# Block-sparse attention with channel mix on one core: another fixed order of the same 2139 operations

## The chip, the cores and the metric

One core of a Trainium2 chip runs the kernel in one launch. The metric is the device time of one execution in microseconds (us), the median over runs. Engines are called as the profile calls them: PE (TensorE), DVE (VectorE), ACT (ScalarE), POOL (GpSimd) and SP (SyncE, which here only issues transfers).

## The reference

What is computed, cut to its core:

```python
scores = scale * q @ k.T            # batch 4, heads 8, sequence 768, head size 64
mask = window(+-1 block of 32) | first/last block row | first/last block column | 3 drawn blocks per row
attn = exp(where(mask, scores, -1e9) - max); attn = attn / (sum(attn) + 1e-9)
x = (attn @ v) as [4, 768, 512]
x_prev = x shifted by one token
xk = mu_k * x + (1 - mu_k) * x_prev;  xr = mu_r * x + (1 - mu_r) * x_prev
k = maximum(xk @ w_k, 0);  v = (k * k) @ w_v      # w_k 512x1024, w_v 1024x512, w_r 512x512
out = sigmoid(xr @ w_r) * v
```

## The kernel before

The sequence has 24 blocks of 32 tokens. The attention is cut into 26 units. Units 0 to 21 ("near") are block rows 1 to 22, each for all four batches: eight blocks of keys (window, first and last block, three drawn ones). Units 22 to 25 ("wide") are the first and last block row of one batch each, against the whole sequence.

A near unit goes through these steps, each one an entry of the plan: its query tile (L305), one new window block of keys (L284) and three drawn blocks (L332) are loaded by SP into slots of a resident tile `KA`, the values in the same way into `VA` (L297, drawn ones L349). PE computes scores in two halves (L402), DVE the row maxima (L412, `nm`), ACT the exponentials (L452, `p`), DVE transposes blocks of 32 (L455, `r`), SP moves the result between partitions by four DMAs (L463, "move", `pt<-r`), PE multiplies with the values (L475). Units 0 to 3 transpose on PE instead (L371, values at L436). Wide units do the same at L496 (scores), L526 (move) and L538 (values), with their own keys (L310) and values (L314). Then the division (L557, L567), a transpose (L576), another move (L581, `xm<-rx`) and a copy into the token tile `xt` (L586, L587, "put x").

The channel mix runs over twelve tiles of 256 tokens, in the order 1 to 10, 0, 11. For each: the two token-shift mixes (L666 on ACT, then L673 on DVE or L669 and L670 on POOL), split into a high and a low part so that three matmul passes give the product (L685, L688, L689); the gate r (L716, in halves `r<t>_0` and `r<t>_1`), the hidden layer h (L737, four pieces `h<t>_0` to `h<t>_3`, ReLU at L752, square and split at L753 to L760), the sigmoid (L805), the values v (L772, eight matmul groups a piece), the product (L778) and the store (L781). The weights come as 64-bit numbers, 0.52 MB a tile (L187, `raw<-w_k` and the like), and are split on chip (around L246).

Nothing is scheduled by a tool. The program builds a list `plan.ops` of 2139 operations, and `Plan.order` hands them out in the sequence of the table `ORDER`; each engine executes its own operations in just that sequence, and waits at an operation until its inputs and its buffers are ready. SP's list is such a sequence too: a move that waits for a transpose holds back all loads behind it. The table `CHOICE` says, by the name of an operation, which engine does it, where several can (`choose`):

```python
def order(self):
    assert sorted(ORDER) == list(range(len(self.ops)))
    return [self.ops[i] for i in ORDER]
...
engine, ns, port, fn = ways[CHOICE.get(name, 0)]
```

`KA` and `VA` are used as rings: a load into a slot has to wait until the unit that read the slot has done so. `r` and `pt` have few buffers, so a unit's transposes follow the move of the one before.

Of the kernel before, what the change touches and what calls it, by code (L numbers as in the profile page):

```python
# [95 lines left out]
def block_sparse_attention_channel_mix(  # L96
# [770 lines left out]
}  # L867
ORDER = [
# [130 lines left out]
```

## Time and profile before

| | us |
|---|---|
| median of 3 runs | 519.79 |
| lowest and highest | 517.22, 520.74 |
| profiled execution | 523.44 |
| its span | 521.7 |
| PE busy in the span | 481.9 (92%) |
| DVE, ACT, POOL busy | 314.0, 306.2, 229.9 |
| mean granted clock of PE | 0.98 |

The span is what the hardware profiler saw of one execution, from the first to the last instruction; the execution's own time is 1.74 us more. The profiled execution lies 3.65 us above the median. A row of a timeline has the start, the length, the engine with the line of the kernel, the output and the input, and in brackets how long the engine stood idle before it and what ended that. A row of a table of waits has the waiting engine and line, what released it, the sum, the count and the longest.

### The profile page before, as it was taken

How to read it: one execution, taken by the hardware profiler on the slowest of the kernel's cores; microseconds unless marked ns; L12 is line 12 of the kernel's file. 1: busy time of each engine (PE TensorE's matmuls, PEld its weight loads, DVE VectorE, ACT ScalarE, POOL GpSimd, SP SyncE). 2: the span in 40 equal slices, each digit the busy share in tenths (PEclk: the TensorE clock that was granted, in tenths of full speed). 3: DMA queues.
4: the chain of work that ended last, by engine and by line, in shares of the span. 5: the costliest groups of instructions: out<-in, count | busy, mean ns of one | idle time of the engine just before them, and what ended most of it. 6: DMA issues, size and time to landing. Idle time of an engine off the chain costs nothing.

```text
span 521.7 us, 18117 instructions
## 1 busy us (share of the span) xinstructions
PE 481.9 (92%) x7384; PEld 400.6 (77%) x7384; DVE 314.0 (60%) x588; ACT 306.2 (59%) x701; POOL 229.9 (44%) x299
## 2 busy tenths in 40 slices
PE   4576789999999899999998999999999999999997
PEld 4254569779788679778877878888679779889896
DVE  3676979884865556674656577584765644624221
ACT  2886979775676645574673646654555645444350
POOL 2425445354443752653672613315264342247641
PEclk9688999999999999999999999999999999999999
DMA  7999999888988888897889789988966853110011
GB/s 267 368 336 338 336 346 280 262 275 219 261 262 216 222 250 249 235 293 229 237 243 255 224 222 266 278 257 257 309 184 175 252 130 78 35 62 0 1 41 40
DMA packets 58052, 114.65 MB, mean 220 GB/s; under 512 B 7665, under 2 KB 20721, under 8 KB 55026
## 3 DMA queue, kind: packets, MB, share of 16 engines
q1 hardware_dynamic: 57970, 113.50, 72.0%
q8 instruction: 58, 0.95, 0.8%
q14 instruction: 24, 0.20, 0.1%
HBM read 77.82 MB, written 6.29 MB: 161 GB/s over the span
## 4 chain that ended last, share of the span: by engine, by line
PE 57%; DMA 10%; SPq 9%; ACT 8%; DVE 6%; POOL 5%; issue 5%; POOLq 0%; DVEq 0%; ACTq 0%
PE v L772 13%; PE h_0p L737 6%; PE h_3p L737 5%; PE s L402 5%; PE h_1p L737 5%; PE h_2p L737 4%; DMA VA<-vt 4%; PE r_0p L716 4%; PE r_1p L716 4%; SPq L463 4%; PE o L475 3%; DMA KA<-kt 3%; PE sw L496 2%; DMA pt<-r 2%; DVE r L455 2%
## 5 line engine op out<-in xcount | busy, mean ns | idle before, releaser
L772 PE MATMUL v<-w,k 128*128 128x512 f32 (+1 forms) x600 | 138.8, 385 | 0.8 <-POOL w L246 0.8
L772 PEld LDWEIGHTS v<-w,k 128*128 128x128 f32 x600 | 108.1, 188 | 28.3 <-issue 5.5
L412 DVE TENSOR_REDUCE nm<-s 128x4 f32<-128x1024 f32 x44 | 52.8, 1214 | 25.4 <-PE s L402 25.2
L402 PE MATMUL s<-KA,q 64*32 64x256 f32 x1408 | 49.2, 408 | 18.6 <-DMA raw<-w_k 10.8
L452 ACT ACTIVATE p<-s,nm 128x256 f32<-128x256 f32 x144 | 60.0, 476 | 0.5
L402 PEld LDWEIGHTS s<-KA,q 64*32 64x32 f32 x1408 | 27.6, 113 | 33.4 <-issue 14.4
L455 DVE STREAM_TRANSPOSE r<-p 128x1024 f32<-128x1024 f32 x36 | 43.7, 1230 | 5.5 <-DMA pt<-r 3.5
L475 PEld LDWEIGHTS o<-VA,pt 128*32 128x32 f32 x2304 | 34.2, 109 | 8.7 <-issue 4.4
L475 PE MATMUL o<-VA,pt 128*32 128x65 f32 x2304 | 37.6, 221 | 2.6 <-DMA VA<-vt 1.4
L716 PE MATMUL r_0p<-w,xr 128*128 128x512 f32 x144 | 36.5, 399 | 1.6 <-issue 1.6
L737 PE MATMUL h_3p<-xk,w 128*128 128x256 f32 x288 | 38.0, 284 | 0.0
L737 PE MATMUL h_1p<-xk,w 128*128 128x256 f32 x288 | 37.9, 283 | 0.1
L737 PE MATMUL h_2p<-xk,w 128*128 128x256 f32 x288 | 37.5, 283 | 0.6 <-issue 0.6
L737 PE MATMUL h_0p<-xk,w 128*128 128x256 f32 x288 | 36.9, 282 | 0.1
L737 PEld LDWEIGHTS h_3p<-xk,w 128*128 128x128 f32 x288 | 35.5, 190 | 1.9 <-issue 1.4
L737 PEld LDWEIGHTS h_1p<-xk,w 128*128 128x128 f32 x288 | 35.7, 189 | 1.5 <-issue 0.4
L716 PE MATMUL r_1p<-w,xr 128*128 128x512 f32 x144 | 36.7, 399 | 0.0
L737 PEld LDWEIGHTS h_2p<-xk,w 128*128 128x128 f32 x288 | 35.5, 190 | 1.5 <-issue 1.2
L737 PEld LDWEIGHTS h_0p<-xk,w 128*128 128x128 f32 x288 | 35.4, 189 | 1.5 <-issue 0.4
L716 PEld LDWEIGHTS r_0p<-w,xr 128*128 128x128 f32 x144 | 26.1, 188 | 8.6 <-issue 2.9
L666 ACT ACTIVATE xr_0d<-xt,mk 128x128 f32<-128x128 f32 x48 | 19.3, 401 | 20.3 <-DVE xr_0f L673 11.5
L716 PEld LDWEIGHTS r_1p<-w,xr 128*128 128x128 f32 x144 | 26.1, 188 | 6.1 <-issue 0.4
(239 smaller groups left out, 833.1 us busy)
## 6 DMA issues: line engine op xcount, KB each, us to landing
VA<-vt SPq DMA_DIRECT2D x92, 260.0 KB, 4.3
KA<-kt SPq DMA_DIRECT2D x89, 256.0 KB, 4.5
pt<-r SPq DMA_DIRECT2D x72, 256.0 KB, 5.0
VA<-vw SPq DMA_DIRECT2D x24, 260.0 KB, 4.1
KA<-kq SPq DMA_DIRECT2D x16, 384.0 KB, 6.1
ptw<-rw SPq DMA_DIRECT2D x32, 192.0 KB, 3.9
out<-z SPq DMA_DIRECT2D x23, 256.0 KB, 4.0
q<-qt SPq DMA_DIRECT2D x22, 256.0 KB, 4.6
```

The costliest lines, as they stand in the source:

```text
L402: nc.tensor.matmul(s.ap[ROWS[j], row, a * 256 : (a + 1) * 256].rearrange("p (n x) -> p n x", x=BLK), q.ap[half, (hp * QB + j) * BLK : (hp ...
L412: nc.vector.tensor_reduce(out=nm.ap.rearrange("p (r a) -> p r a", r=2), in_=s.ap.rearrange("p r (a x) -> p r a x", a=2), axis=AX.X, op=ALU ...
L452: plan.add(f"u{name} exp {i}", ACT, 365, lambda row=row, a=a, i=i: nc.scalar.activation(squares()[:, :, :, i, :], s.ap[:, row, a * 256 : ( ...
L455: plan.add(f"u{name} turn", DVE, N_TURN, lambda: nc.vector.transpose(out=r.ap[:, :, gi].rearrange("p j c i x -> p j (c i x)"), in_=squares ...
L463: nc.sync.dma_start(pt.ap[:, b].rearrange("p g c i x -> p (g c i x)"), r.ap[ROWS[b]].rearrange("p j g c i x -> p j (g c i x)"))
L475: nc.tensor.matmul(o[gi].ap[ROWS[j], i * DV : (i + 1) * DV], pt.ap[:, j, gi, g, 2 * row + a, :], VA.ap[:, c0 + g, j, h * DV : (h + 1) * DV ...
L496: nc.tensor.matmul(s.ap[HALF[a], row, 0:W], q.ap[half, 2 * hp * BLK : 2 * (hp + 1) * BLK], wide_keys(b, hp)[half, k * W : (k + 1) * W], st ...
L666: nc.scalar.activation(parts(d.ap), cols(c, 0), AF.Copy, scale=mk.ap[:, which, c : c + 1])
L716: nc.tensor.matmul(pr.ap[:, 0:512], xr.ap[:, a, c, :], weight_of["r", c].ap[:, w, :], start=(c == 0 and m == 0), stop=(c == CC - 1 and m = ...
L737: nc.tensor.matmul(ph.ap[:, ff * TT : (ff + 1) * TT], weight_of["k", c, f2 // 2].ap[:, w, f % 4 * P : (f % 4 + 1) * P], xk.ap[:, a, c, :], ...
L772: nc.tensor.matmul(pv.ap[:, 0:width], k2.ap[:, a, f, i * P : (i + 1) * P], weight_of["v", f].ap[:, w, cs], start=(f == 0 and m == 0), stop ...
```

## The change

Only the tables `CHOICE` and `ORDER` differ. The 2139 operations, their buffers, the bytes they move and PE's 7384 matmuls are the same. 244 operations run on another engine; among them, 27 mixing operations (net) go from POOL to DVE. The order changes nearly everywhere. One line of each table:

```diff
 CHOICE = {
...
-    "u9 put x": 1, "u10 put x": 1, "u15 put x": 1, "u16 put x": 1, "u17 put x": 1, "u18 put x": 1, "u19 put x": 1, "u21 put x": 1, "w0 tail": 2, "w0 lo": 1, "w1 tail": 2,
...
+    "u7 put x": 1, "u9 put x": 1, "u10 put x": 1, "u11 put x": 1, "u12 put x": 1, "u14 put x": 1, "u15 put x": 1, "u20 put x": 1, "w0 tail": 2, "w0 lo": 1, "w1 tail": 2,
...
 ORDER = [
-    2, 0, 7, 3, 16, 11, 4, 994, 13, 1, 973, 924, 926, 14, 931, 925, 934, 932, 5, 12, 55, 927, 928, 974, 933, 935, 996, 10, 936, 937, 15, 34, 6, 995, 966, 8, 929, 930, 56, 18,
+    0, 2, 10, 3, 16, 994, 11, 7, 14, 952, 959, 12, 973, 4, 995, 1, 55, 15, 953, 954, 955, 996, 956, 961, 962, 997, 980, 960, 56, 945, 998, 963, 8, 964, 18, 957, 965, 5, 958,
```

Three places in the order follow. A name such as `s12_0` is the first half of unit 12's scores, `r3_1p` the second gate half of tile 3, `pt14` the moved tile of unit 14, `raw3` the loaded weight tile number 3.

First PE, at the scores of unit 12. Before:

```order
L737 MATMUL h3_2p_2992<-xk3_2374,w9_1134 128x256 x3
L737 MATMUL h3_2p_2992<-xk3_2374,w10_540 128x256 x3
L737 MATMUL h3_2p_2992<-xk3_2374,w11_371 128x256 x3
L402 MATMUL s12_0_3031<-KA_67,q12_2627 32x256 x16
L402 MATMUL s12_1_3048<-KA_67,q12_2627 32x256 x16
L716 MATMUL r3_1p_3065<-w0_643,xr3_1_2773 128x512 x3
L716 MATMUL r3_1p_3065<-w1_290,xr3_1_2773 128x512 x3
L716 MATMUL r3_1p_3065<-w2_252,xr3_1_2773 128x512 x3
L716 MATMUL r3_1p_3065<-w3_749,xr3_1_2773 128x512 x3
```

After the change:

```order
L737 MATMUL h3_2p_2957<-xk3_2355,w11_339 128x256 x3
L716 MATMUL r3_1p_3007<-w0_660,xr3_1_2712 128x512 x3
L716 MATMUL r3_1p_3007<-w1_577,xr3_1_2712 128x512 x3
L716 MATMUL r3_1p_3007<-w2_764,xr3_1_2712 128x512 x3
L716 MATMUL r3_1p_3007<-w3_565,xr3_1_2712 128x512 x3
L772 MATMUL v3_1_0_3043<-w12_1267,k23_2819 128x512 x3
L402 MATMUL s12_0_3054<-KA_67,q12_2905 32x256 x16
L402 MATMUL s12_1_3074<-KA_67,q12_2905 32x256 x16
L772 MATMUL v3_1_0_3043<-w13_1347,k23_2819 128x512 x3
```

The gate half `r3_1` and a first group of `v3_1` now stand ahead of the scores, where they stood behind them.

Second SP, around the values of unit 14. Before, a store, the move of unit 14, a store, and then its drawn values (L349, three blocks):

```order
L781 DMA out<-z4_0_3471 128x512
L463 DMA pt14_4080<-r14_3935 128x1x512 x4
L781 DMA out<-z3_1_3088 128x512
L349 REGISTER_ALU x2
L349 ISA
L349 DMA VA_68<-vt 32x2080
L349 REGISTER_ALU x2
L349 ISA
L349 DMA VA_68<-vt 32x2080
L349 REGISTER_ALU x2
L349 ISA
L349 DMA VA_68<-vt 32x2080
```

After the change, the move of unit 13, a query, and then the drawn values of unit 14:

```order
L463 DMA pt13_3674<-r13_3620 128x1x512 x4
L305 DMA q15_3718<-qt 128x512
L349 REGISTER_ALU x2
L349 ISA
L349 DMA VA_68<-vt 32x2080
L349 REGISTER_ALU x2
L349 ISA
L349 DMA VA_68<-vt 32x2080
L349 REGISTER_ALU x2
L349 ISA
L349 DMA VA_68<-vt 32x2080
```

The drawn values of unit 14 went from behind its own move to right behind the move of unit 13; its own move stands 28 rows further on.

Third SP at the start, from a drawn block of keys to the first drawn block of values of unit 0. Before:

```order
L332 DMA KA_67<-kt 128x512
L297 DMA VA_68<-vt 32x2080
L305 DMA q1_331<-qt 128x512
L187 DMA raw10_359<-w_k 128x1024
L297 DMA VA_68<-vt 32x2080
L284 DMA KA_67<-kt 128x512
L187 DMA raw3_366<-w_r 128x1024
L187 DMA raw6_369<-w_k 128x1024
L349 REGISTER_ALU x2
L349 ISA
L349 DMA VA_68<-vt 32x2080
```

After the change:

```order
L187 DMA raw4_276<-w_k 128x1024
L297 DMA VA_68<-vt 32x2080
L159 DMA mk_70<-mu_k 128x4
L305 DMA q1_289<-qt 128x512
L297 DMA VA_68<-vt 32x2080
L187 DMA raw1_316<-w_r 128x1024
L284 DMA KA_67<-kt 128x512
L187 DMA raw2_351<-w_r 128x1024
L187 DMA raw3_354<-w_r 128x1024
L349 REGISTER_ALU x2
L349 ISA
L349 DMA VA_68<-vt 32x2080
```

Between the two, four weight tiles (L187) are loaded where there were three, and one of the constants comes in between.

## Rows read from the trace of the kernel before

**Rows 1.** The page, part 1: busy time, share of the span, instructions of each engine

```profile
PE 481.9 (92%) x7384; PEld 400.6 (77%) x7384; DVE 314.0 (60%) x588; ACT 306.2 (59%) x701; POOL 229.9 (44%) x299
```

**Rows 2.** Busy time by stretch: length, engines, granted clock, DMA share, GB/s

```profile
0.00:78.00 78.00, 51.89 (x1148) 37.41 (x1149) 52.56 (x100) 55.31 (x127) 33.02 (x42) 0.87 0.93 332
...
130.00:330.00 200.00, 192.78 (x3300) 161.60 (x3289) 126.54 (x238) 118.74 (x282) 96.35 (x124) 1.00 0.86 245
...
416.00:522.00 106.00, 102.18 (x896) 89.28 (x884) 39.58 (x75) 43.30 (x94) 43.87 (x60) 1.00 0.18 48
```

**Rows 3.** PE's waits from 78 us on: total us, times, longest

```profile
PE s L402 <- DVE rx L576: 2.0, 1, 2.0
PE s L402 <- DMA KA<-kt: 1.5, 1, 1.5
PE o L475 <- DMA VA<-vt: 1.4, 3, 0.6
PE sw L496 <- ACT h_2k L752: 1.2, 1, 1.2
PE o L475 <- DMA pt<-r: 1.2, 3, 0.6
PE s L402 <- ACT z L805: 0.9, 1, 0.9
PE v L772 <- POOL w L246: 0.8, 1, 0.8
PE h_2p L737 <- issue: 0.6, 1, 0.6
PE s L402 <- DMA VA<-vt: 0.4, 1, 0.4
```

**Rows 4.** PE's timeline, first 78 us: start, us, instruction, [idle before]

```profile
31.55 3.48 PE L436 MATMUL o<-VA,pt 128*32 128x65 f32 x128 [2.86 <-DMA VA<-vt]
...
40.11 0.63 PE L402 MATMUL s<-KA,q 64*32 64x256 f32 x5 [1.02 <-issue]
...
72.40 0.64 PE L402 MATMUL s<-KA,q 64*32 64x256 f32 x8 [1.96 <-issue]
```

**Rows 5.** Waits of SP's queue, 130 to 330 us, first and last of 16

```profile
SPq L581 <- ACT xk L688: 1.8, 2, 1.4
...
SPq L349 <- DMA KA<-kt: 0.2, 1, 0.2
```

**Rows 6.** PE's timeline, from 165 to 345 us

```profile
174.07 3.05 PE L716 MATMUL r_1p<-w,xr 128*128 128x512 f32 x12
...
195.91 1.96 PE L402 MATMUL s<-KA,q 64*32 64x256 f32 x64 [0.42 <-DMA VA<-vt]
...
211.49 1.96 PE L402 MATMUL s<-KA,q 64*32 64x256 f32 x64
...
323.96 2.02 PE L475 MATMUL o<-VA,pt 128*32 128x65 f32 x128
...
338.18 2.03 PE L475 MATMUL o<-VA,pt 128*32 128x65 f32 x128
```

**Rows 7.** SP's timeline, from 190 to 364 us: when transfers are issued

```profile
211.87 4.41 SPq L463 DMA_DIRECT2D pt<-r  x4
...
231.54 3.99 SPq L463 DMA_DIRECT2D pt<-r  x4
...
318.06 0.93 SPq L297 DMA_DIRECT2D VA<-vt  x1
...
328.54 4.07 SPq L463 DMA_DIRECT2D pt<-r  x4
...
360.32 1.82 SPq L310 DMA_DIRECT2D KA<-kq  x2
```

**Rows 8.** The page, part 6: transfers: count, KB each, median us to landing

```profile
VA<-vt SPq DMA_DIRECT2D x92, 260.0 KB, 4.3
...
pt<-r SPq DMA_DIRECT2D x72, 256.0 KB, 5.0
```

184 rows, old and new, of tables (CHOICE, ORDER) are left out of this document.

## Prediction

> **What bounds the kernel now.** I read the page first. TensorE (PE) is busy for 92% of the span, VectorE (DVE) for 60%, ScalarE (ACT) for 59%, GpSimd (POOL) for 44% [rows 1]. So the end is set by PE's list of matmuls, which is the same before and after, plus the time in which PE stands. The busy time by stage shows where it stands: 51.9 of the first 78 us are busy, 192.8 of the 200 us from 130 to 330, 102.2 of the last 106 [rows 2]. The sixteen DMA engines are 93% busy in the first stretch, 86% in the second, 18% in the last: what comes after 416 us has its data already.
>
> PE's waits from 78 us on come next: nine, together 10.0 us [rows 3]. That is all that an order can win behind 78 us. In the first 78 us PE is idle for 26 us; that part is a race for bytes (332 GB/s), and there are four gaps with no releaser, together 7.2 us the first and the last of them: [rows 4].
>
> Last I looked at SP, which issues all transfers in one fixed list. In the 200 us from 130 to 330 SP's queue waits 16 times, 10.3 us in sum, the longest line 1.8 us and the shortest 0.2 the first and the last of them: [rows 5]. For the other 190 us it issues or is between issues. PE and SP are thus both nearly full there, and SP's list holds the same transfers after the change.
>
> **The change, part by part.** The profiled execution took 523.44 us, 1.74 more than its span of 521.7 and 3.65 more than the median 519.79. I work out a difference on the span and take it off both.
>
> *Waits that the new order covers.* The scores of unit 12 waited 2.0 us the first of [rows 3]; in the new PE list twelve gate matmuls (3.05 us at 174.07, [rows 6]) and a piece of v stand ahead of them, so the 2.0 go. The scores of unit 18 waited 1.5 us for their keys [rows 3]; now the two halves of a hidden piece come first, and SP has the keys ahead of the move of unit 16: 1.5 go. The wide scores of unit 23 waited 1.2 us [rows 3]; the row names ACT, but the last pair of their keys was issued at 360.32 [rows 7], and with a few us to land it is as late as ACT; one of the pair moves far forward in SP's list: 1.2 go. The scores of unit 15 (0.9, for ACT), a v piece (0.8, for a POOL weight split) and an issue gap (0.6) [rows 3] all meet other neighbours: I count these 2.3 as gone, but any of them can come back elsewhere. The waits for values and moves (1.4, 1.2 and 0.4, [rows 3]) I count at half, 1.5 gone, since most feeds of units 9 to 18 get 1.5 to 3 us more between issue and use, but the traffic stays dense. Sum: 2.0 + 1.5 + 1.2 + 2.3 + 1.5 = 8.5 us.
>
> *What SP gives back.* If PE comes 8.5 us earlier to the last near units, SP must be there as well. For unit 19 the last value feed is issued at 318.06, takes 4.3 us to land [rows 7, 8], so is there at 322.4, and PE uses it at 323.96 [rows 6]: 1.6 us spare. For unit 20 the move's four issues start at 328.54 and end at 332.6; with 5.0 us to land that is 337.6 against 338.18 [rows 6 to 8]: 0.6 spare. The new list shifts drawn values and moves there, which I read as worth a few us either way and cost at nothing. I take 1.6, the first. SP itself can shrink only by its waits, 10.3 us at most [rows 5], since the DMAs are the same; they are mostly for DVE and ACT work, which comes earlier if PE does. Bounds: nothing saved gives back 8.5 - 1.6 = 6.9, all saved gives back 0. I take a third saved, 3.4, as most of the sixteen waits are under 0.5 us and only shift: back 8.5 - 1.6 - 3.4 = 3.5 us.
>
> *The start.* Counted from the two lists, the bytes ahead of the first scores are equal (4.3 MB). Ahead of unit 0's drawn values one more weight of 0.52 MB is loaded; at 332 GB/s [rows 2] that is 1.6 us later, and the wait for it, 2.86 us [rows 4], grows by as much. Further on, units 3 and 4 pay about as much again, but by unit 7 both lists have loaded the same, so most is repaid: I take +0.5, bounds -1.5 and +2.5.
>
> *Engines.* 27 mixing operations go from POOL to DVE net, and splits and copies go round among three engines. Each engine stands at least 40% of the span [rows 1]; I cost it at nothing. Without that cover one late piece costs PE what such waits cost before, 0.8 to 1.2 us [rows 3]. Behind 416 us only the order of v pieces and splits differs: nothing, bounds -0.5 and +0.5.
>
> *The issue gaps.* Counted in the trace, the four early gaps lie 256 PE instructions apart or a multiple of that, with DMA 93% busy [rows 2, 4]; both lists cross these points in the same crowded stretch, so I leave the 7.2 us as they are. The Trainium skill ("Runtime: NRT & Kernel Launch", section "Instruction fetch mechanics") says that an engine refills its instructions in blocks of 256 by sequential prefetch and that crossing a block is mostly hidden. The row agrees on the 256, not on hidden, as long as DMA is full; if the rule held with an order that keeps DMA less full there, the sum would be 7.2 lower.
>
> Sum: -8.5 + 3.5 + 0.5 = -4.5 us. Span 517.2, profiled execution 518.9, median 519.79 - 4.5 = 515.3.
>
> **Rivals.**
> 1. *All waits go.* SP's waits melt with PE's, and nothing is given back: -10.0 + 0.5 = -9.5, median 510.3. For it: most feeds are earlier against their use. Against: SP would have to lose nearly all of its 10.3 us, and the three groups of feed waits to vanish at 86% DMA. Should the early gaps shrink too, it goes as low as 507.
> 2. *The waits only move.* SP saves nothing: -8.5 + 6.9 + 0.5 = -1.1, and with one new late piece (0.8 to 1.2) it is 0: median 519 to 520. For it: 190 of 200 us of SP are not waits. Against: its waits are for work that would come earlier.
> 3. *SP stalls at moves, slower.* The scores of units 14, 15 and 18 are put later on PE and their moves earlier on SP. Unit 14's scores started at 211.49 and ended 1.96 later; its move was issued at 231.54 [rows 6, 7], 18.1 us behind. With the PE work of the new order, counted in durations of the trace, 8.9 us are left; for unit 15 11.6, for unit 18 12.9. Unit 13, with scores from 195.91 and its move at 211.87 [rows 6, 7], took 14.0 for the same chain of two reductions, eight exponentials and two transposes. If the three take 14.0 as well, SP, which runs strictly in order, stands 5.1 + 2.4 + 1.1 = 8.6 us with the feeds of the next units behind it. Then PE at unit 19 is late by 8.6 - 1.6 + 0.5 = 7.5, and all that was won is lost: 527.3. If SP saves its third it is 523.9. It decides once the stalls exceed the spare plus what SP's own waits save, 1.6 + 3.4 = 5.0 us. Against it: DVE and ACT are busy for 127 and 119 of these 200 us [rows 2], so the chain can run faster when it comes first in their lists; unit 14 had its 18.1 us because nothing pressed.
>
> **How the numbers follow.** Forecast (SP gives back part): 0.48. Rival 1: 0.22, rival 2: 0.13, rival 3: 0.17. One per cent, 5.2 us, is about what a measurement of this kernel tells from no change, so faster means below 514.6. The forecast lies at 515.3 and is cut by that bound: 0.16 faster, 0.32 same. Rival 1 is all faster; rival 2 all same; rival 3 goes 0.14 slower (above 525.0), 0.03 same. Faster 0.38, same 0.48, slower 0.14. The range reaches to rival 1 with some of the early gaps, 508, and into rival 3, 525; the forecast's own is 512 to 518.5.
>
> **What would show it.** Right: no wait of 1 us or more ahead of the scores of units 12 and 18 or the wide scores of unit 23; PE's waits between 78 and 300 us fall to some 3 us in sum, new waits for VA or pt appear near units 19 to 21, and SP's waits from 130 to 330 fall to about 7. The wait ahead of unit 0's values grows from 2.86 to about 4.4. Wrong on the fast side: no new waits there. Wrong on the slow side: SP waits of over 2 us for DVE's transposes at the moves of units 14, 15, 18, with PE waiting for VA or KA right behind. The whole sum is off if the first 78 us move by more than 2 us, for which I have only the bytes to go by.

## The result, and the profile after

The changed kernel takes 525.43 us in the median (521.37 to 529.49, 14 runs), the kernel before 520.48 us in the 14 runs beside it. The ratio is 1.0092, 95% interval 1.0066 to 1.0117: about 4.8 us slower. Medians, here and below, are over all executions, ratios and intervals over those within 1.5% of the fastest of their kernel. The forecast was 515.3, and the top of its range, 525, lies just below the result. The profiled execution took 529.03 us with a span of 527.3, 5.6 us longer than that of before.

Part 1 of the page of the changed kernel, against [rows 1]:

```profile
PE 484.5 (92%) x7384; PEld 401.9 (76%) x7384; DVE 321.6 (61%) x611; ACT 303.9 (58%) x695; POOL 210.2 (40%) x255
```

Busy time by stretch (columns as in [rows 2]):

```profile
0.00:78.00 78.00, 48.20 (x1112) 34.11 (x1112) 51.07 (x99) 47.34 (x109) 29.80 (x35) 0.82 0.90 314
...
130.00:330.00 200.00, 193.78 (x3300) 162.65 (x3300) 133.69 (x253) 117.83 (x282) 76.91 (x96) 1.00 0.85 244
...
416.00:528.00 112.00, 108.21 (x1013) 94.52 (x1011) 42.97 (x80) 51.00 (x110) 44.59 (x55) 1.00 0.20 53
```

The first stretch is where it went: PE is busy for 48.2 instead of 51.9 of the first 78 us, and the transfers run at 314 instead of 332 GB/s, with the DMA share at 0.90 instead of 0.93. From 130 to 330 us PE is as busy as before: 193.8 against 192.8.

PE's waits from 78 us on, against [rows 3]:

```profile
PE o L475 <- DMA VA<-vt: 2.7, 4, 1.2
PE s L402 <- DMA pt<-r: 1.3, 1, 1.3
PE sw L496 <- DMA KA<-kq: 1.3, 2, 0.9
PE s L402 <- DMA KA<-kt: 1.1, 1, 1.1
PE s L402 <- ACT xr L688: 1.0, 1, 1.0
PE h_2p L737 <- ACT xt L614: 0.8, 1, 0.8
PE h_0p L737 <- issue: 0.5, 1, 0.5
PE h_0p L737 <- DVE z L778: 0.4, 1, 0.4
PE s L402 <- issue: 0.3, 1, 0.3
PE r_1p L716 <- ACT h_2k L752: 0.3, 1, 0.3
PE h_0p L737 <- ACT xt L614: 0.2, 1, 0.2
```

They sum to 9.9 us, where before it was 10.0. Not one of the big entries is the old one: the 2.0 ahead of unit 12's scores, the 1.5 ahead of unit 18's and the 1.2 ahead of the second part of unit 23's are gone, and as much stands elsewhere. The entries of 1 us and more are now at the scores of units 11, 13 and 19 (1.32, 1.04, 1.15) and at the values of unit 16 (1.18).

PE's timeline of the first 78 us, against [rows 4]:

```profile
32.02 1.96 PE L436 MATMUL o<-VA,pt 128*32 128x65 f32 x64 [2.83 <-DMA VA<-vt]
35.39 1.96 PE L436 MATMUL o<-VA,pt 128*32 128x65 f32 x64 [1.41 <-ACT pt L375]
...
50.40 0.42 PE L436 MATMUL o<-VA,pt 128*32 128x65 f32 x12 [4.12 <-issue]
...
64.12 1.10 PE L402 MATMUL s<-KA,q 64*32 64x256 f32 x32 [1.54 <-DMA VA<-vt]
```

The wait for unit 0's first values is 2.83 us, as before (2.86). Its second half, which before followed at once, now waits for a copy by ACT; later there are a longer issue gap (4.12) and a wait ahead of unit 4's scores. The waits of SP's queue from 130 to 330 us, of 13 lines the first and the last ([rows 5] answers to it):

```profile
SPq L581 <- DVE rx L576: 3.1, 1, 3.1
...
SPq L297 <- PE s L402: 0.2, 1, 0.2
```

They sum to 10.5 us (10.3 before). At the moves of the units (L463) the three lines are 0.6, 0.4 and 0.3, so the stalls there that rival 3 feared didn't come; the 3.1 us are at a move of x (L581) before 180 us.

### The profile page after: what moved, and what is told of

The parts are those of the page before. It is cut to its first block, busy times and chain, and to the rows that moved or that the text cites. A ratio compares the mean times of both kernels' runs of the same rounds, so it can differ in the third digit from the quotient of the medians.

```text
span 527.3 us, 18088 instructions
## 1 busy us (share of the span) xinstructions
PE 484.5 (92%) x7384; PEld 401.9 (76%) x7384; DVE 321.6 (61%) x611; ACT 303.9 (58%) x695; POOL 210.2 (40%) x255
## 4 chain that ended last, share of the span: by engine, by line
PE 49%; SPq 16%; DVE 8%; DMA 7%; issue 6%; ACT 6%; POOL 3%; DVEq 0%; ACTq 0%; POOLq 0%
PE v L772 13%; SPq L463 5%; PE h_1p L737 5%; PE r_0p L716 4%; PE h_0p L737 4%; PE h_2p L737 4%; PE h_3p L737 4%; PE r_1p L716 4%; PE s L402 3%; SPq L349 3%; SPq L581 2%; PE o L538 2%; PE sw L496 2%; DMA KA<-kq 2%; SPq L332 2%
## 5 line engine op out<-in xcount | busy, mean ns | idle before, releaser
L416 ACT ACTIVATE nm<-nm 128x4 f32<-128x4 f32 x44 | 8.9, 201 | 42.9 <-DVE nm L412 42.9
```

## The experiments

All times are medians of runs beside runs of the kernel before on the same chip; ratios are to those. In the diffs of lists of operations, a list is a piece of one engine's order, by the plan's names.

**Which half costs.** Two kernels join the two orders at one place, where both have done almost the same operations; engines are taken from the kernel whose order is followed.

```diff
 e1_old_start_new_rest
-ORDER = before
+ORDER = before[:552] + [i for i in changed if i not in before[:552]]
 e2_new_start_old_rest
+ORDER = changed[:552] + [i for i in before if i not in changed[:552]]
```

> Order and engines of the first 552 operations from the kernel before (up to unit 6's values on PE, some 115 us), all others in the changed kernel's order and on its engines. Theory A (the new start costs it all, the new rest is worth nothing, as PE's waits behind 78 us sum to 10.0 us in the one and 9.9 in the other): within 1.5 us of before, first gate half of tile 2 within 1 us of before's start. Rival B (the new rest is worth the 4 us that were forecast, the late start hides it): 4 us faster than before. Rival C (the loss is in the rest): 4 to 5 us slower than before.

> The other way round: first 552 operations of the changed kernel's order, the rest in the order of before. Theory A: 4 to 6 us slower than before, like the changed kernel. Rival B: 8 to 9 us slower. Rival C: within 1.5 us of before.

Old start, new rest: 521.08 us, ratio 0.9988 (0.9957 to 1.002). New start, old rest: 528.17 us, 1.0122 (1.0083 to 1.016). Theory A holds: the loss is in the start. The new rest is worth nothing that these runs can tell: by the interval of e1 between 2.2 us gained and 1.0 us lost, where the forecast had 5.0 gained behind the start. The traces say the same. Unit 7's scores on PE, in the kernel before, e1, the changed kernel and e2, one fence each:

```profile
101.50 1.96 PE L402 MATMUL s<-KA,q 64*32 64x256 f32 x64
```
```profile
101.29 1.96 PE L402 MATMUL s<-KA,q 64*32 64x256 f32 x64
```
```profile
107.19 1.96 PE L402 MATMUL s<-KA,q 64*32 64x256 f32 x64 [0.30 <-issue]
```
```profile
105.34 1.96 PE L402 MATMUL s<-KA,q 64*32 64x256 f32 x64
```

With spans of 521.7, 521.6, 527.3 and 526.3, what follows takes 420.2, 420.3, 420.1 and 421.0 us. The difference is complete at 107 us, and neither rest makes it up.

A trace is one execution, and executions of one order differ by more than these four suggest. The run m1 below has the start of the kernel before, and its row of unit 7's scores is

```profile
98.12 1.96 PE L402 MATMUL s<-KA,q 64*32 64x256 f32 x64
```

3.4 us earlier. What follows unit 7 takes from 414.5 us (n2) to 421.0 (e2) in sixteen traces of the runs here. On average the two rests are alike: 418.9 us in the seven with the old one (before, e2, s6, b1, b3, b4, n3) and 418.3 in the nine with the new one (changed, e1, s1 to s5, n1, n2). PE's waits behind 78 us sum to between 5.2 and 10.7 in the seven, 8.9 on average, and to between 5.6 and 10.3 in the nine, 8.5 on average. The unmended starts stay apart: 98.1 to 101.5 in the three traces with the old one, 105.3 and 107.2 with the new one. So differences of under some 3 us between two single traces mean little below; the ratios decide.

**Cutting the start earlier.**

```diff
 e3_old_25us
+ORDER = before[:78] + [i for i in changed if i not in before[:78]]
 e4_old_50us
+ORDER = before[:186] + [i for i in changed if i not in before[:186]]
```

> Only the first 78 operations from before (to the first scores of unit 1, some 25 us), all others in the changed kernel's order. If the loss lies in the loads ahead of the first scores and the lower clock that follows (theory A1): within 2 us of before, unit 6's second scores at 88 to 90 us. If it lies between 25 and 80 us, in the order of weights, values and exponentials (A2): 4 to 5 us slower than before, unit 6's second scores at 93 us or later.

> The first 186 operations from before (to unit 2's values on SP, some 50 us), all others in the changed kernel's order. A1 and A2 (the loss lies ahead of 50 us): within 2 us of before. If units 3 to 6 bring the loss (A3): 3 us or more slower than before.

e3 takes 535.17 us (1.026, 1.0207 to 1.0314), outside both of its expectations. e4 takes 529.78 (1.0153, 1.0102 to 1.0203); "3 us or more slower" would take that in, but by their ratios both are worse than either parent (e4 with an overlap of intervals), so the cut itself seems to cost, and e4 says nothing for A3. At 552 operations the two orders have done the same but for three on each side; at 78 they differ in 21, at 186 in 16. They take the weight tiles in different sequences, so behind the cut the lists hold weight steps whose data is not there yet, ahead of the units' steps. In e3, PE's timeline, and behind it the first step of ACT after 24.1 us:

```profile
38.31 1.96 PE L402 MATMUL s<-KA,q 64*32 64x256 f32 x32 [12.47 <-ACT p L423]
...
47.96 1.96 PE L436 MATMUL o<-VA,pt 128*32 128x65 f32 x64 [5.08 <-ACT pt L375]
```
```profile
32.95 0.67 ACT L201 ACTIVATE wmag<-raw 128x512 f32<-128x512 f32 x1 [8.85 <-DMA raw<-w_k]
```

ACT stands 8.85 us at a weight step, for its bytes, and PE waits 12.47 us for ACT's exponential behind it and later 5.08 for ACT's copy. The runs don't place the loss, but show what a weight step in front of a unit's step in an in-order list can cost.

**The changed kernel, mended piece by piece.** Its trace has three things in the start that before has not. On POOL a copy of a key slot (L293) stands behind three weight steps. On DVE three more weight steps stand ahead of unit 1's first row maximum and a fourth ahead of the second. ACT's copy of unit 0's last transposed tile stands behind the two negations that wait for these maxima, as it did before, but the negations now wait 1.93 and 2.15 us, and two exponentials and two weight steps stand between them and the copy. ACT's timeline in the changed kernel:

```profile
30.30 0.20 ACT L416 ACTIVATE nm<-nm 128x4 f32<-128x4 f32 x1 [1.93 <-DVE nm L412]
32.66 0.21 ACT L416 ACTIVATE nm<-nm 128x4 f32<-128x4 f32 x1 [2.15 <-DVE nm L412]
...
34.77 0.57 ACT L375 COPY pt<-t0 0 0_453 128x512 f32<-128x512 f32 x1
```

Before, that copy ran at 30.31:

```profile
30.31 0.55 ACT L375 COPY pt<-t0 0 0_425 128x512 f32<-128x512 f32 x1
```

And on SP unit 5's drawn keys stand ahead of unit 3's drawn values, which are issued from 59.61 us on instead of 53.76. The mends:

```diff
 s1_key_copy_first: POOL
-u1 keys again 3, w5 tail, w6 tail, w6 lo, u0 keys again 4
+u1 keys again 3, u0 keys again 4, w5 tail, w6 tail, w6 lo
 s2_tops_before_weights: DVE, then ACT
-w4 tail, w4 sign, w4 join, u1 1 top, w1 sign, u1 0 top
+u1 1 top, u1 0 top, w4 tail, w4 sign, w4 join, w1 sign
-u1 1 less, u1 0 less, u1 0 exp 2, w1 size, u1 1 exp 2, w3 size, u0 0 0 turned
+u0 0 0 turned, u1 1 less, u1 0 less, u1 0 exp 2, w1 size, u1 1 exp 2, w3 size
 s3_u3_values_first: SP
-u4 q, u4 drawn keys, u5 drawn keys, u4 keys 4, u3 drawn values, u3 values 1 2
+u4 q, u4 drawn keys, u4 keys 4, u3 drawn values, u3 values 1 2, u5 drawn keys
 s4_all_three: s1, s2 and s3;  s5_tops_and_u3: s2 and s3
```

> The changed kernel with one operation moved: POOL's copy of a key slot for unit 0 (L293) goes back ahead of three weight steps on POOL. If that copy releases the first scores (theory A1a): the scores of unit 0 start at 17.1 us instead of 18.0; total 0.5 to 1 us less than the changed kernel, some 524.5 us. If the first scores wait for bytes (the forecast's way of counting): still 18.0, no change.

> The changed kernel with unit 1's two row maxima on DVE ahead of four weight steps, and on ACT the copy of unit 0's last transposed tile ahead of unit 1's negations and exponentials. If these engine queues delay unit 0's values (theory A1b): the second values of unit 0 start at 34 us instead of 35.4 without a wait for ACT's copy, unit 1's values at 42 to 43 instead of 44.4; total 1 to 2 us less than the changed kernel, 523.5 to 524.5. If the start is bound by bytes: same starts within 0.5 us, same time.

> The changed kernel with unit 5's drawn keys on SP behind unit 3's values, as before, instead of ahead of them. If the late values of unit 3 matter (theory A2): the second values of unit 3 start 1.5 to 2 us earlier than 73.2 us, total about 524. If PE is late there already for other reasons: less than 0.5 us.

> All three moves on the changed kernel. If they are the cause of the late start: unit 6's second scores at 89 to 90 us instead of 94.3 (before: 88.4), total 520.5 to 522, as before within 1.5 us. If the gains don't add or lie elsewhere (other engines, the granted clock): 523 or more.

> The changed kernel with the moves of row maxima and copies (DVE, ACT) and of unit 5's keys (SP), but POOL's key copy left where the change put it. If that copy never mattered: the same as with all three moves, 521.5 to 523, unit 5's second values at 95 to 96 us. If it did: 1 us more than with all three.

| | us | ratio, interval | unit 7's scores in its trace |
|---|---|---|---|
| changed | 525.43 | 1.0092, 1.0066 to 1.0117 | 107.19 |
| s1 | 527.05 | 1.0112, 1.007 to 1.0155 | 109.47 |
| s2 | 524.77 | 1.006, 1.0024 to 1.0095 | 103.18 |
| s3 | 524.1 | 1.0052, 1.0015 to 1.009 | 103.80 |
| s4 | 522.67 | 1.0028, 1.0 to 1.0057 | 102.55 |
| s5 | 524.69 | 1.0084, 1.0056 to 1.0113 | 101.81 |

The key copy alone is a miss: the first scores did start at 17.07 us in s1, but they start at 17.03 in e2 too, whose start is the changed one, so the 18.00 of the changed kernel's trace is a matter of the execution, and the time didn't fall. s2 takes away the wait it was made for (PE's timeline, s2; both halves of unit 0's values in one row):

```profile
31.47 2.11 PE L436 MATMUL o<-VA,pt 128*32 128x65 f32 x128 [1.65 <-DMA VA<-vt]
```

It and s3 bring unit 7's scores 3 to 4 us forward in the trace (e2, with the changed start as it is, 1.9), but of the time they show only 0.3 to 0.4%, and their intervals overlap that of the changed kernel. The three together bring back two thirds of the loss, and the interval of s4 lies below that of the changed kernel. s5 misses by its time (1.0084) though its profiled start is as early as that of s4: the sizes of the parts don't add, and the runs can't say whether the key copy has a share after all.

**The forecast's waits, alone.** The three waits that the forecast named, treated on the kernel before:

```diff
 m1_three_waits: PE, PE, SP
-u12 0 scores, u12 1 scores, r3_1 0, r3_1 1
+r3_1 0, r3_1 1, u12 0 scores, u12 1 scores
-u18 0 scores, u18 1 scores, h6_0 0, h6_0 1
+h6_0 0, h6_0 1, u18 0 scores, u18 1 scores
-u22 wide keys 0 1, u23 wide keys 0 0
+u22 wide keys 0 1, u23 wide keys 0 0, u23 wide keys 1 0
```

> The kernel before with three of its waits treated alone: unit 12's scores behind the gate half r3_1, one hidden piece ahead of unit 18's scores, the late pair of unit 23's wide keys moved forward on SP. The forecast's theory: the waits of 2.0, 1.5 and 1.2 us go, about half comes back at units 19 to 21, so 1.5 to 3 us less than before. Rival (the waits only move, since PE and SP are both full there): they go, as much appears within the next units, total within 1 us of before.

519.83 us, ratio 0.9995 (0.9965 to 1.0024): the rival rather than the forecast, whose smallest gain, 1.5 us, is just inside the interval. PE's timeline of m1 shows an exchange. Unit 12's scores run at 169.88 without a wait, and unit 10's values behind them wait for a feed:

```profile
169.88 1.96 PE L402 MATMUL s<-KA,q 64*32 64x256 f32 x64
...
175.79 2.03 PE L475 MATMUL o<-VA,pt 128*32 128x65 f32 x128 [3.04 <-DMA VA<-vt]
```

That feed was issued late in SP's list (SP's timeline, m1), right behind a move:

```profile
165.31 4.01 SPq L463 DMA_DIRECT2D pt<-r  x4
169.37 0.60 SPq L297 DMA_DIRECT2D VA<-vt  x1
```

It took 6.3 us to land, where the median was 4.3 [rows 8]. The 2.0 us of before are paid six microseconds later as 3.04, and a wait of 1.94 appears at a wide scores step at 336 us. The waits of this trace behind 78 us sum to 8.0, inside the range of the old rest above: the trace shows where waits came back, and only the ratio says that the time didn't fall.

**Parts of the change on the kernel before.**

```diff
 b1_weight_ahead: SP
-u0 drawn values, u0 values 1 3, u0 values 1 1, u2 drawn keys, u2 keys 5, u2 q, w0 load
+w0 load, u0 drawn values, u0 values 1 3, u0 values 1 1, u2 drawn keys, u2 keys 5, u2 q
 b2_keys_ahead: SP
-u4 drawn keys, u4 keys 4, u3 drawn values, u3 values 1 2, w12 load, u5 q, u5 drawn keys
+u4 drawn keys, u5 drawn keys, u4 keys 4, u3 drawn values, u3 values 1 2, w12 load, u5 q
 b3_tops_late: DVE, then ACT
-u1 1 top, u1 0 top, w10 join, w6 tail
+w10 join, w6 tail, u1 1 top, u1 0 top
-w6 sign, u0 0 0 turned, u1 1 exp 3, u1 1 exp 2, w3 sign
+w6 sign, u1 1 exp 3, u1 1 exp 2, w3 sign, u0 0 0 turned
 b4_tops_and_keys: b2 and b3
```

> The kernel before with one more weight tile of 0.52 MB loaded ahead of unit 0's drawn values. The forecast's way of counting bytes: unit 0's first values at 33.1 us instead of 31.55, total 0.5 to 1.5 us more than before. If the start is paced by the engines and not by bytes: values later by less than 0.5 us, total the same.

> The kernel before with unit 5's drawn keys on SP ahead of unit 4's last keys and unit 3's values, as in the changed kernel. If the order of feeds there is half of the loss (A2): unit 3's second values at 69 to 70 us instead of 67.4, total 1 to 2.5 us more than before. If it is not: the same within 0.5 us at unit 3, and total the same.

> The kernel before with what the change did on DVE and ACT at units 0 and 1, alone: three weight steps on ACT and two on DVE ahead of unit 1's row maxima, and ACT's copy of unit 0's last transposed tile behind two exponentials and a weight step. If the queues of DVE and ACT are a part of the loss: unit 0's second values at 34 to 35 us instead of 33.3, PE waits there for ACT's copy, total 0.5 to 2 us more than before. If not: within 0.5 us of before.

> The kernel before with both: the moves of the run with late row maxima, and unit 5's drawn keys ahead of unit 3's values on SP. If these two make the most of the changed kernel's loss: unit 5's second values at 98 to 101 us instead of 94.7, total 3 to 5 us more than before. If other parts of the new start do (weights loaded in another order, other engines): less than 2 us more.

b1: 522.1 us, 1.0029 (0.9996 to 1.0062). Unit 0's values start at 33.19 us, as the count of bytes had it, with a wait of 3.45 (PE's timeline, b1); in six traces in which these loads stand as before (before, e1, m1, b3, b4, n3) they start at 31.27 to 31.94:

```profile
33.19 3.48 PE L436 MATMUL o<-VA,pt 128*32 128x65 f32 x128 [3.45 <-DMA VA<-vt]
```

So the price of the bytes, 1.6 us, is about right on the kernel before, though the wait grew by only 0.6. In the changed kernel it was not paid: this wait didn't grow. b2: 522.54, 1.0029 (0.9995 to 1.0062). b3: 520.37, 0.9993 (0.9954 to 1.0031): a miss; the new wait there is only 0.53 us in its trace, not the 1.41 of the changed kernel. Its edit adds two weight steps ahead of the row maxima, where the change added four. b4: 523.3, 1.0055 (1.0024 to 1.0086): the feeds and the queues together rebuild some 0.55 of the 0.92%, less than was expected of them, and unit 5's second values come at 94.68 in its trace, not at 98 to 101.

**The mended start with the old rest.** The two mends of s5 on e2:

```diff
 s6_mended_start_old_rest
+ORDER = e2's, with the moves of s2 and s3
```

> The new start with row maxima, copies and unit 5's keys put back in place (two of the three mends, POOL's key copy left), and the old order for all else. If the start is the cause and these two mend the most of it: 520 to 523 us, where the new start unmended with the old rest gave 528. If the rest of the new start costs as much by itself: 525 or more.

523.91 us, 1.0086 (1.0049 to 1.0124): between the two expectations. Of the 1.22% of e2 it takes off a third, with overlapping intervals, as s5 takes off little.

**SP stands at a load.** In all new starts up to here unit 1's values begin at 44 us or later. The waits of SP's queue in the first 90 us, before (first lines):

```profile
SPq L284 <- PE s L402: 4.4, 3, 3.5
SPq L297 <- PE o L436: 3.7, 3, 3.3
```

and in the changed kernel:

```profile
SPq L297 <- PE o L436: 7.6, 3, 3.5
SPq L284 <- PE s L402: 6.0, 2, 3.7
```

SP waits 3.9 us longer at loads of values (L297) for PE to finish the values of units 0 to 3 (L436) that still read the slot. One of these loads is unit 1's window block, with three drawn blocks queued behind it; SP's timeline in the changed kernel:

```profile
32.30 1.54 SPq L284 DMA_DIRECT2D KA<-kt  x1
37.19 0.47 SPq L297 DMA_DIRECT2D VA<-vt  x1
38.02 2.28 SPq L349 DMA_DIRECT2D VA<-vt  x3
```

From 33.84 to 37.19 it stands. Before, the drawn blocks came first, and SP stood for 0.3 us there:

```profile
32.63 2.12 SPq L349 DMA_DIRECT2D VA<-vt  x3
34.98 0.49 SPq L297 DMA_DIRECT2D VA<-vt  x1
```

But PE's own row of unit 1's values in the changed kernel names another wait, for ACT's copy of the transposed tile:

```profile
44.37 1.91 PE L436 MATMUL o<-VA,pt 128*32 128x65 f32 x116 [0.68 <-ACT pt L375]
```

```diff
 n1_u1_drawn_values_first: SP, in the changed kernel
-u2 keys 5, u1 values 1 0, u1 drawn values
+u2 keys 5, u1 drawn values, u1 values 1 0
 n2_all_mends: n1, s2 and s3
 n3_rebuilt_on_before: b4, and on SP
-u1 drawn values, u1 values 1 0
+u1 values 1 0, u1 drawn values
```

> The changed kernel with one swap on SP: unit 1's drawn values ahead of its window values, as before. In the changed kernel SP stood 3.35 us ahead of the window values (their slot is free only when unit 0's values are done), with the drawn values queued behind. If this is the main stall of the new start: unit 1's values start at 42 to 43 us instead of 44.4, unit 5's second values at 96 to 98 instead of 98.7 to 102.4, total 1.5 to 3 us less than the changed kernel, 522.5 to 524. If not: the same within 1 us.

> The changed kernel with that swap, the row maxima and copies put back, and unit 5's keys behind unit 3's values. If SP's stalls and the queues of DVE and ACT are the whole cause: unit 5's second values at 93 to 95 us, total as before within 1.5 us, 519.5 to 522. If other parts of the new start cost as well: 523 or more.

> The kernel before with the three moves that are under suspicion and nothing else of the change: unit 1's window values ahead of its drawn values, unit 5's drawn keys ahead of unit 3's values, row maxima and ACT's copy late. If they are the cause: 523.5 to 526, like the changed kernel, unit 1's values at 44 us or later. If the loss needs the rest of the new start: as without the swap, 523 or less.

n1: 524.87 us, 1.0072 (1.0039 to 1.0106): alone it isn't it. Unit 1's values start at 45.80, behind ACT's copy with 0.68 us of wait, as in the changed kernel; SP's stall was not what they waited for. n2: 522.55, 1.0014 (0.9975 to 1.0053; by the medians alone 1.0035): with these three mends the changed kernel can't be told from the one before, and its rest is the new one. Its unit 1's values come at 44.21, so they are not where it gains; unit 4's first scores start at 57.00 instead of 64.12, but at 57.80 in s5 as well, whose time is 1.0084. n3: 523.09, 1.0058 (1.002 to 1.0097): no more than b4.

So three moves in the start undo the loss (n2), or with the key copy as the third two thirds of it (s4), and their like put on the kernel before makes 0.6 of the 0.9% (n3). All of these move operations within an engine's list; no operation changes its engine. What each is worth by itself stays open: the single steps of 0.2 to 0.4% are inside the intervals, and why two of the mends without a third (s5) take back so little the traces don't show. No version beat the kernel before beyond its interval.

## Why the prediction was wrong

Two terms of the sum failed, and each makes about half of the 9.3 us between the forecast of -4.5 and the measured +4.8.

**The start** was put at +0.5, with +2.5 as the upper bound, "for which I have only the bytes to go by". With the old rest behind it (e2) the new start costs 1.22%, 6.4 us (4.3 to 8.3 by the interval); on PE's timeline it is 5.7 us at unit 7's scores (107.19 - 101.50). The extra weight tile was counted rightly, nine tiles ahead of unit 0's drawn values instead of eight, but its price is not what the changed kernel paid: the wait there is 2.83 us, not the 4.4 that were to show it, and the values start at 32.02 (31.29 in e2, with the same start) against 31.55. From 13 to 26 us the transfers ran at 391 GB/s where before it was 367. What was not looked at is what stands in front of unit 0's to 3's steps in the in-order lists of DVE, ACT and SP: weight steps ahead of row maxima, a load that waits for a slot ahead of loads that could go, another unit's keys ahead of values that PE needs. That such places make the loss n2 shows; which of them how much stays open. *Engines* were costed at nothing with their idle 40% as cover; that share is a mean, and in the start the order within the list decided. The prediction's own sign, "the first 78 us move by more than 2 us", came true.

**What the middle wins and SP gives back** was put at -8.5 + 3.5 = -5.0. Measured it is -0.6 us (-2.2 to +1.0, e1): SP gives back all of what is won, or nearly. The named waits went as forecast (units 12, 18 and 23), but the sum stayed at 9.9, and with those waits alone taken away m1 is no faster: SP issues for some 175 of the 200 us, in the kernel before, the changed one and m1 alike, and an earlier PE can meet the next feed instead. At one feed m1 shows that; for the other waits it is argued. That is rival 2 for the middle, which had 0.13. The forecast expected the new waits near units 19 to 21; in m1 the largest came 6 us behind the one taken away, and in the changed kernel those of 1 us and more are at units 11, 13, 16 and 19. The base was weak as well: the 10.0 us were those of one execution, and other traces with the same rest have 5.2 to 10.7. The nine waits of PE and the sixteen of SP are lines of a table; they stand for 13 and 19 waits.

**Rival 3** had 523.9 to 527.3, and the result lies there by luck, for its stalls at the moves didn't come. Unit 14's scores on PE and its move on SP in the changed kernel:

```profile
223.99 1.96 PE L402 MATMUL s<-KA,q 64*32 64x256 f32 x64
```
```profile
236.56 4.28 SPq L463 DMA_DIRECT2D pt<-r  x4
```

The move was issued 10.6 us behind the end of the scores, not the 14.0 that unit 13 had taken, and SP's waits show nothing at it: the chain of reductions, exponentials and transposes was faster when it had to be. SP standing in front of an operation that isn't ready, with feeds queued behind, is real at a load in the start (3.35 us up to 37.19), though unit 1's values didn't wait for it.

**The issue gaps** were left as they are. In the changed kernel's trace that held in sum, the row of 4.12 with two more of 1.05 and 1.33 making 6.5 against 7.2, but this is luck: the same gaps sum to 5.4 us in e1 and 2.0 in m1, which have the start of before, to 3.6 in e2, which has the new one, and s4 shows none. **Behind 416 us** nothing was expected; in sum both rests take 420 to 421 us in the four traces compared above.

## What to carry to other kernels

Where one engine is nearly full and its supplier too, a wait that an order removes can come back at the next feed, as here; count on a gain only if the supplier has slack at the same place. Take the waits that a forecast is to remove from several executions, for one execution's waits are partly its own. Read a new order in the crowded stretch first, list by list: for each step that the bottleneck waits for, what now stands ahead of it on its own engine, and whether that can be ready. To find which part of a reordering costs, join the two orders at a place where both have done nearly the same operations: two runs split the result, while a cut where they have not (e3, e4) makes a cost of its own.

## What the runs showed of the hardware

PE's granted clock was lower in parts of the new starts, but the runs don't show that this made the loss. From 13 to 26 and from 26 to 39 us (last three columns: granted clock, DMA share, GB/s), before, in the changed kernel, and in n2 for the first of the two stretches:

```profile
13.00:26.00 13.00, 7.18 (x108) 3.78 (x116) 8.74 (x12) 10.77 (x23) 6.19 (x7) 0.63 0.97 367
26.00:39.00 13.00, 9.64 (x251) 6.88 (x236) 9.21 (x19) 11.23 (x24) 3.75 (x3) 0.80 0.96 338
```
```profile
13.00:26.00 13.00, 6.00 (x84) 3.29 (x92) 7.99 (x11) 8.04 (x18) 7.73 (x8) 0.63 1.02 391
26.00:39.00 13.00, 8.77 (x204) 6.60 (x188) 7.77 (x11) 8.56 (x21) 4.37 (x6) 0.63 0.91 331
```
```profile
13.00:26.00 13.00, 7.34 (x92) 4.20 (x100) 6.96 (x10) 8.03 (x19) 7.79 (x8) 0.50 1.04 396
```

In n2 the clock was 0.50, the lower of the two levels (1.2 of 2.4 GHz), from 13 to 26 us, behind 10.26 us in which PE had nothing to do, and a group of four transposes took 1.11 us there instead of 0.66. Yet n2 is as fast as the kernel before. The same 7384 matmuls took 484.5 us of busy time in the changed kernel against 481.9, but 484.1 in e1 and 485.7 in n2, with spans of 521.6 and 516.4.

The gaps without a releaser, which the prediction found 256 PE instructions apart, differ from execution to execution: the one in unit 1's values is 2.60 us before, 4.12 in the changed kernel and 0.35 in e2, which has the same start as the changed kernel.
